# Attention of the first stretches in single fp32 matmuls instead of high and low halves

## The chip, the cores and the metric

The kernel runs on one core of a Trainium2 chip. The metric is the device time of one execution in microseconds (us). An execution's profile shows the span from the first to the last instruction on five engines: PE (TensorE, matrix products into PSUM), DVE (VectorE), ACT (ScalarE), POOL (GpSimd) and SP (SyncE, which here only issues DMAs). PEld is the weight load of PE.

## The reference

Causal attention with a bias, then two feed-forward layers whose activations differ. Batch 4, 8 heads, 576 queries, head size 64; 2304 tokens of width 512, feed-forward width 2048.

```python
scores = (q @ k.T) / sqrt(64)
cum = cumsum(maximum(s, 0))
bias = -(cum[:, None] - cum[None, :])
scores = where(causal, -1e9, scores + minimum(bias, 0))
x = softmax(scores) @ v              # heads side by side: 2304 x 512
h = x @ w_in;  g = maximum(h, 0) + log1p(exp(-abs(h)));  x = g @ w_out
h = x @ w_in2; g = P(h) / (Q(h) + 1e-6);                 out = g @ w_out2
```

P is a cubic and Q a quadratic with coefficients from the inputs. The weights arrive as 64-bit floats.

## The kernel before, in words

**Halves.** Every product is made precise by splitting its operands: hi is the value rounded to the short matmul format (F32R, written by an ACT copy), lo the rest (a subtraction on DVE or POOL). A feed-forward product takes three matmuls, hi x hi, hi x lo and lo x hi (L670 to L672, and L706 to L708). For scores, q and k (64 rows) are loaded twice, onto 128 partitions; `ht` holds hi and lo stacked for k and hi twice for q, `st` the lo of q against the hi of k, with four rows more for the bias: cum in high and low parts, and ones. So a score block takes two matmuls, of 128 and of 68 rows (L318, L319). The bias enters in the sum, q.k + 8 (cum_k - cum_q), and the mask in the softmax. V is stored as hi and lo side by side (`vs`), and the transposed P as two tiles, `pt_h` and `pt_l`, so that PV takes each block of P twice; its two 64-row results are added at the end by an ACT copy (L429) and a DVE add (L430). Matmuls of halves are given at least 256 columns, where need be with columns of zeros (the first 192 of each P tile, zeroed at L833).

**Parts.** A head's queries are cut into parts: M (queries 0 to 255), B (256 to 383), L (0 to 383) and H (384 to 575). The order (L444 to L450): batch 0's eight M, batch 0's eight pairs B and H, batch 1's eight L; then batch 1's H and batch 2's L, and last batch 2's H with batch 3's L and H. Each part goes through load_raw (DMAs of q, k and V), prep (halves), s1 and s2 (scores and softmax), t1 and t2 (transposes on PE through `ident`, evacuation), and pv. The loop at L464 to L485 writes them out as one stream, in which load_raw of a part stands two parts ahead, prep one, t1 and t2 one behind, pv two behind.

In softmax (L296 to L315) DVE adds the mask and takes the minimum, ACT takes the exponential with its sum, DVE the reciprocal, POOL multiplies P by it.

**The feed-forward part and the weights.** Layer one works on token tiles of 256, 256 and four of 448, with 16 slices ff of the width. A unit is a tile and a slice: 12 matmuls into h (L670 to L672), the activation on ACT and DVE, halves of it on ACT and POOL (L800, L802), 12 matmuls into the accumulators (L706 to L708). The two tiles of 256 share accumulators; a matmul with zeros opens each of these (L690). A weight slice is converted in two pieces per slice from 64-bit numbers: POOL (L536), ACT (L537), DVE (L538, L543), ACT (L547) and POOL (L548), from a load on SP's queue (L521); the low half is also stored to DRAM (L557) and read back when a later tile needs it (L567).

**What sets the order.** Tile's scheduler keeps each engine's program order, shifted by priorities (`ahead`); every engine takes its instructions in that order. `run_to` lets the stream of parts go on between units by fixed fractions (`GROUPS`, L913): batch 0's M parts run before the first unit, with conversions in their later half; batch 0's B and H parts within units 0 to 7, batch 1's L parts within units 8 to 31. All loads named here are on SP's one queue, in order.

**The start.** load_s0 and make_cum0 (L156 to L175) make batch 0's bias rows: DVE takes the maximum and the running sum (L166, L167), splits it (L168, L169), mixes the parts (L170, L171); ACT writes two rows each (L174); eight small DMAs put them into `st` (L215). prep_hi and prep_lo (L231 to L238) make halves of q and k by pairs of heads; the first two pairs at once, the other two before their parts. make_cum (L184 to L199) does the same for all rows and stores them in DRAM (`cum_d`), from where prep loads them by L275.

**Buffers.** `W` has 16 buffers of 4 KB per partition for weights and start tiles, `Q` 6 (raw, ht, st), `J` 4 (the P tiles), `V` 2 (vs), `R` 2 (raw V, later weights and results).

Of the kernel before, what the change touches and what calls it, by code (L numbers as in the profile page):

```python
# [54 lines left out]
def moe_chain_kernel(ctx, tc, qk0, qk, vv, s0, s, w1, w2, ab, out):  # L55
# [62 lines left out]
    class Part:  # L118
        def __init__(self, b, h, kind, rng, first):
            self.b, self.h, self.kind, self.rng = b, h, kind, rng  # L120
            self.fresh, self.first = rng is not None, first
# [7 lines left out]
    raw2, ht2, st2 = {}, {}, {}  # L129
# [26 lines left out]
    def load_s0():  # L156
        cum_t["s0"] = t_w("s0_t", [4 * H, M + 6], F32)
        nc.sync.dma_start(out=cum_t["s0"], in_=s0)

    def make_cum0():  # L160
        st, cst = cum_t["s0"][:, 0:M], cum_t["s0"][:, M:M + 6]
        one = t_w("one", [4 * H, M], F32)
        nc.vector.memset(one, 1.0)
        t = t_w("cum0", [4 * H, 4, M], F32)
        hi = t_w("cum0h", [4 * H, M], F32R)
# [40 lines left out]
    def open_pair(i):  # L206
        ht2[i] = t_w("ht2", [128, 2, 2, M], F32R)
        st2[i] = t_w("st2", [128, 2, 2, M], F32R)

    def load_cum(i):  # L210
        if i not in ht2:
            open_pair(i)
        for j in range(2):
            h = 2 * i + j
            nc.sync.dma_start(out=f(st2[i][64:68, j]), in_=f(cum_t["c"][4 * h:4 * h + 4]))  # L215

    def load_v0():
        t = t_r("v2", [128, 4, 2, 2, D], F32)
# [5 lines left out]
    def prep_v0(i):  # L224
        vr = v2["raw"][:, 2 * i:2 * i + 2].rearrange("p r c h d -> p (r c) h d")
        vs = t_v("vs2", [128, 4, 4, D], F32R)
        nc.scalar.activation(vs[:, :, 0:4:3, :], vr, AF.Copy)
        nc.vector.tensor_tensor(vs[:, :, 1:3, :], vr, f(vs[:, :, 0:4:3, :]), op=ALU.subtract)
        v2[i] = vs

    def prep_hi(i):  # L231
        nc.scalar.activation(ht2[i], raw2[i], AF.Copy)
        nc.scalar.activation(st2[i][0:64, :, 1], raw2[i][0:64, :, 1], AF.Copy)

    def prep_lo(i):
        raw, ht, st = raw2.pop(i), ht2[i], st2[i]
        nc.vector.tensor_tensor(st[0:64, :, 0], raw[0:64, :, 0], f(ht[0:64, :, 0]), op=ALU.subtract)
        nc.vector.tensor_tensor(ht[64:128, :, 1], raw[64:128, :, 1], f(ht[64:128, :, 1]), op=ALU.subtract)  # L238

    def prep_pair(i):  # L240
        if i > 1:
            prep_hi(i)
            prep_lo(i)
        ht, st = ht2.pop(i), st2.pop(i)
        if i == 2:
            prep_v0(1)
        for j in range(2):
            op_t[0, 2 * i + j] = (ht[:, j], st[:, j], v2[i // 2][:, (i % 2) * 2:(i % 2) * 2 + 2])

    def load_raw(p):  # L250
        if p.fresh:
            raw = t_q("raw", [128, 2, S], F32)
            nc.sync.dma_start(out=cols(raw, p.rng), in_=cols(qk[p.b, p.h], p.rng))
            raw_t[p] = raw
            p.vkey = (p.b, p.h // 2, p.rng)
            if p.vkey not in v_t:
                n = -(-p.rng[1] // 128) if p.rng[0] == "pre" else 5
                vr = tmp_tile("R", 2, (128, 5, 2, D))
                nc.sync.dma_start(out=vr[:, 0:n], in_=vv[p.b, p.h // 2, :, 0:n])
                v_t[p.vkey] = [vr, None, n]  # L260

    def prep(p):
# [3 lines left out]
        elif p.fresh:  # L266
# [50 lines left out]
    def scores(o, p, q0, k0, n):  # L317
        nc.tensor.matmul(o, p.ht[:, 0, q0:q0 + 128], p.ht[:, 1, k0:k0 + n], start=True, stop=False)  # L318
# [12 lines left out]
    def s1(p):  # L331
        p.stat = sb.tile([128, 3, 4], F32, tag="stat", bufs=3, name="stat")
        if p.kind in "LM":
            p.p1 = p_tile(p, "gh")
            bk = abank()
            scores(bk[:, 0:256], p, 0, 0, 256)
            scores(bk[:, 256:512], p, 128, 0, 256)
            softmax_rows(p.p1, bk, 0, 128, p.stat, 0)
            softmax_rows(p.p1[:, 128:384], bk[:, 256:512], 128, 256, p.stat, 1)
# [20 lines left out]
    def evac_pt(dst, src):  # L360
# [4 lines left out]
    def t1(p):  # L365
        p.ph, p.pl = pt_h[p.idx % 2], pt_l[p.idx % 2]
# [3 lines left out]
        if p.kind in "LM":  # L370
            for i, c0 in enumerate((256, 0, 128)):
                nc.tensor.transpose(bk[:, i * 128:(i + 1) * 128], p.p1[:, c0:c0 + 128], ident)
            evac_pt([t[:, 192:576] for t in (p.ph, p.pl)], bk[:, 0:384])
        else:
            for c in range(4):
                nc.tensor.transpose(bk[:, c * 128:(c + 1) * 128], p.p1[:, c * 128:(c + 1) * 128], ident)
            evac_pt(
                [t[:, 256:1024].rearrange("p (c q) -> p c q", c=4)[:, :, 0:128] for t in (p.ph, p.pl)],
                bk.rearrange("p (c q) -> p c q", c=4))

    def t2(p):
# [3 lines left out]
        if p.kind in "LB":  # L385
            for i in range(3):
                nc.tensor.transpose(bk[:, i * 128:(i + 1) * 128], p.p2[:, i * 128:(i + 1) * 128], ident)
            evac_pt([t[:, 576:960] for t in (p.ph, p.pl)], bk[:, 0:384])
        else:

            for i, k0 in reversed(list(enumerate((448, 0, 128, 256, 384)))):
                nc.tensor.transpose(bk[:, i * 64:(i + 2) * 64], p.p2[:, k0:k0 + 128], ident)  # L392
            evac_pt(
                [t[:, 64:1024].rearrange("p (c q) -> p c q", c=5)[:, :, 128:192] for t in (p.ph, p.pl)],
                bk[:, 64:384].rearrange("p (c q) -> p c q", c=5))

    def pv(p):
# [3 lines left out]
        for t in (p.ph, p.pl):  # L401
            if p.kind == "L":
# [24 lines left out]
        cs, qs = slice(c0, c0 + n), slice(q0, q0 + n)  # L427
        tm = tmp_tile("tmp", 1, (128, 384))
# [11 lines left out]
    def parts_of(lst, first=False):  # L440
        return [Part(b, h, k, r, first) for b, heads, kind in lst for h in heads for k, r in SPLIT[kind]]
# [18 lines left out]
    n = 0  # L460
# [222 lines left out]
    def open_acc(ph, T):  # L683
# [122 lines left out]
    if True:  # L806
# [23 lines left out]
        for i in range(2):  # L830
            for lst, nm in ((pt_h, "pth"), (pt_l, "ptl")):
                t = t_j(nm, [128, 1024], F32R)
                nc.gpsimd.memset(f(t[:, 0:192]), 0.0)  # L833
                lst.append(t)
# [217 lines left out]
```

## Time and profile before

| | |
|---|---|
| median of 3 runs | 1104.4 us (1101.86 to 1104.44) |
| span of the profiled execution | 1100.2 us |
| the profiled execution's own time | not given apart from its span |
| PE busy | 1030.3 us (94%), 5732 matmuls |
| PEld busy | 926.5 us (84%) |
| DVE busy | 825.4 us (75%), 1904 instructions |
| ACT busy | 836.6 us (76%), 1767 instructions |
| POOL busy | 488.2 us (44%), 543 instructions |
| DMA | 140.53 MB, mean 128 GB/s |
| granted clock, mean | 0.995 |

Busy time is the union of an engine's instructions; matmuls overlap, so that PE's is more than their number times their pace. "Idle before" is the idle time of the engine just ahead of an instruction, with what ended it. The granted clock is a share of 2.4 GHz.

### The profile page before, as it was taken

How to read it: one execution, taken by the hardware profiler on the slowest of the kernel's cores; microseconds unless marked ns; L12 is line 12 of the kernel's file. 1: busy time of each engine (PE TensorE's matmuls, PEld its weight loads, DVE VectorE, ACT ScalarE, POOL GpSimd, SP SyncE). 2: the span in 40 equal slices, each digit the busy share in tenths (PEclk: the TensorE clock that was granted, in tenths of full speed). 3: DMA queues.
4: the chain of work that ended last, by engine and by line, in shares of the span. 5: the costliest groups of instructions: out<-in, count | busy, mean ns of one | idle time of the engine just before them, and what ended most of it. 6: DMA issues, size and time to landing. Idle time of an engine off the chain costs nothing.

```text
span 1100.2 us, 17835 instructions
## 1 busy us (share of the span) xinstructions
PE 1030.3 (94%) x5732; PEld 926.5 (84%) x5732; DVE 825.4 (75%) x1904; ACT 836.6 (76%) x1767; POOL 488.2 (44%) x543
## 2 busy tenths in 40 slices
PE   3588889889999999999999999899999999999998
PEld 3477778789888888888999998799999999999996
DVE  6898998777888788886556677667777677776765
ACT  6698888878787788777556555688788888888885
POOL 3655576552222122221244676445445455454543
PEclk9999999999999999999999999899999999999999
DMA  6464566466555464432777974401000010000000
GB/s 227 167 221 158 181 222 217 162 205 178 166 160 158 142 205 132 154 94 66 226 235 223 323 280 149 160 1 45 13 30 29 1 58 1 29 30 1 30 1 29
DMA packets 70493, 140.53 MB, mean 128 GB/s; under 512 B 8384, under 2 KB 23904, under 8 KB 70400
## 3 DMA queue, kind: packets, MB, share of 16 engines
q1 hardware_dynamic: 68000, 135.37, 37.5%
q10 hardware_dynamic: 2400, 4.03, 1.5%
q8 instruction: 45, 0.74, 0.3%
q14 instruction: 48, 0.39, 0.1%
HBM read 112.66 MB, written 22.61 MB: 123 GB/s over the span
## 4 chain that ended last, share of the span: by engine, by line
PE 65%; DVE 5%; DMA 3%; ACT 3%; POOL 2%; issue 2%; SPq 0%; POOLq 0%; ACTq 0%; DVEq 0%
PE h L672 6%; PE h L671 6%; PE h L670 6%; PE acc L715 6%; PE acc L714 6%; PE acc L713 6%; PE at L418 3%; PE at L670 3%; PE at L672 3%; PE at L671 3%; PE acc L706 3%; PE acc L707 3%; PE acc L708 3%; PE at L318 2%; DMA raw64x<-in_w_dram 2%
## 5 line engine op out<-in xcount | busy, mean ns | idle before, releaser
L671 PE MATMUL h<-xs,w1h 128*128 128x448 f32 (+1 forms) x352 | 119.9, 341 | 1.4 <-DVE xs L640 1.4
L670 PE MATMUL h<-xs,w1h 128*128 128x448 f32 (+1 forms) x352 | 119.9, 342 | 1.3 <-DVE e L764 1.0
L707 PE MATMUL acc<-gl,w1h 128*128 128x448 f32 (+1 forms) x352 | 119.1, 338 | 1.2 <-POOL gl L802 1.2
L706 PE MATMUL acc<-gh,w1h 128*128 128x448 f32 (+1 forms) x352 | 119.7, 341 | 0.1
L672 PE MATMUL h<-xs,w1l 128*128 128x448 f32 (+1 forms) x352 | 118.8, 338 | 0.2 <-POOL w1l L548 0.2
L708 PE MATMUL acc<-gh,w1l 128*128 128x448 f32 (+1 forms) x352 | 118.4, 336 | 0.0
L715 PE MATMUL acc<-w2h,gl 128*128 128x512 f32 x288 | 113.8, 395 | 0.4 <-POOL gl L802 0.4
L713 PE MATMUL acc<-w2h,gh 128*128 128x512 f32 x288 | 113.8, 395 | 0.4 <-ACT gh L800 0.4
L714 PE MATMUL acc<-w2l,gh 128*128 128x512 f32 x288 | 113.6, 394 | 0.0
L315 POOL TENSOR_SCALAR PA<-PA,stat 128x384 f32<-128x384 f32 (+3 forms) x112 | 69.3, 622 | 97.2 <-DVE stat L314 51.9
L802 POOL TENSOR_TENSOR gl<-PA,gh 128x384 fp32r<-128x384 f32 x96 | 99.4, 1036 | 6.3 <-issue 4.0
L773 POOL TENSOR_TENSOR tc<-tc,e 128x384 f32<-128x384 f32 x48 | 51.7, 1076 | 102.7 <-ACT tc L771 102.7
L315 POOL TENSOR_SCALAR P<-P,stat 128x576 f32<-128x576 f32 x32 | 26.2, 819 | 143.2 <-DVE stat L313 50.7
L363 DVE TENSOR_TENSOR ptl<-at,pth 128x384 fp32r<-128x384 f32 (+2 forms) x108 | 60.7, 569 | 16.3 <-ACT pth L362 15.1
L312 ACT ACTIVATE PA<-PA,stat 128x384 f32<-128x384 f32 (+3 forms) x112 | 63.9, 571 | 10.3 <-DVE stat L299 9.0
L670 PEld LDWEIGHTS h<-xs,w1h 128*128 128x128 f32 x352 | 67.0, 191 | 5.5 <-DVE e L764 1.7
L671 PEld LDWEIGHTS h<-xs,w1h 128*128 128x128 f32 x352 | 66.8, 190 | 5.0 <-DVE xs L640 2.2
L707 PEld LDWEIGHTS acc<-gl,w1h 128*128 128x128 f32 x352 | 66.4, 189 | 4.9 <-POOL gl L802 2.0
L362 ACT ACTIVATE pth<-at 128x384 fp32r<-128x384 f32 (+2 forms) x108 | 53.3, 499 | 21.4 <-PE at L392 12.2
L706 PEld LDWEIGHTS acc<-gh,w1h 128*128 128x128 f32 x352 | 66.4, 189 | 3.6 <-DVE yb L736 0.5
L672 PEld LDWEIGHTS h<-xs,w1l 128*128 128x128 f32 x352 | 66.6, 189 | 3.1 <-POOL w1l L548 0.4
L708 PEld LDWEIGHTS acc<-gh,w1l 128*128 128x128 f32 x352 | 66.2, 188 | 3.0
(225 smaller groups left out, 3311.9 us busy)
## 6 DMA issues: line engine op xcount, KB each, us to landing
w1l<-l_d SPq DMA_DIRECT2D x148, 256.0 KB
raw<-in_w_dram SPq DMA_DIRECT2D x48, 512.0 KB
raw<-in_qk_dram SPq DMA_DIRECT2D x32, 384.0 KB
l_d<-w1l SPq DMA_DIRECT2D x32, 256.0 KB
raw64x<-in_w_dram SPq DMA_DIRECT2D x16, 512.0 KB
R<-in_vv_dram SPq DMA_DIRECT2D x16, 320.0 KB
raw<-in_qk_dram SPq DMA_DIRECT2D x8, 576.0 KB
out_dram<-yb SPq DMA_DIRECT2D x18, 256.0 KB
```

Source lines behind the costliest of these rows:

```text
L312: nc.scalar.activation(pt[:, 0:n], pt[:, 0:n], AF.Exp, bias=mn, scale=-1.0, accum_out=stat[:, i, 1:2])
L315: nc.gpsimd.tensor_scalar(pt[:, 0:n], pt[:, 0:n], stat[:, i, 2:3], 1.0, op0=ALU.mult, op1=ALU.mult)
L670: nc.tensor.matmul(h, wh[:, cs], xh, start=(k == 0), stop=False)
L671: nc.tensor.matmul(h, wh[:, cs], xl, start=False, stop=False)
L672: nc.tensor.matmul(h, wl[:, cs], xh, start=False, stop=(k == KD - 1))
L706: nc.tensor.matmul(o, wh[:, cs], gh, start=first and not both, stop=False)
L707: nc.tensor.matmul(o, wh[:, cs], gl, start=False, stop=False)
L708: nc.tensor.matmul(o, wl[:, cs], gh, start=False, stop=last and (not both or m % 2 == 1))
L713: nc.tensor.matmul(acc[m], gh[:, cs], wh, start=first, stop=False)
L714: nc.tensor.matmul(acc[m], gh[:, cs], wl, start=False, stop=False)
L715: nc.tensor.matmul(acc[m], gl[:, cs], wh, start=False, stop=last)
L802: eng.tensor_tensor(gl, g, f(gh), op=ALU.subtract)
```

## The change

The parts of the first three stretches (M, B and H of batch 0, L of batch 1) become "plain": q, k, V and P stay fp32 and go to the matmul as they are. Scores take one matmul of 66 or 68 rows on the loaded tile, with the bias rows loaded into it below q and k; q and k are loaded onto 64 partitions. Bias rows of the start are two for each head (cum and one) instead of four. V is loaded straight into `V` and used for both heads of a pair; the result is copied from the rows of its head (DVE). P is evacuated once, t1's by ACT and t2's by DVE, into one of four rotating `J` tiles. Column counts are no longer padded: an M or L part's first row block has 128 columns of scores, and PV takes only the columns that the mask leaves. `pt_h` and `pt_l` are made when the first part of halves needs them. The matmul that opens an accumulator multiplies the zero columns of `mask` with `mask`, in fp32.

```diff
 def load_s0():
-        cum_t["s0"] = t_w("s0_t", [4 * H, M + 6], F32)
+        cum_t["s0"] = sb.tile([2 * H, M + 4], F32, tag="tmp", bufs=1, name="s0_t")
...
 def make_cum0():
...
         nc.vector.tensor_tensor_scan(t[:, 1], one, t[:, 0], 0.0, op0=ALU.mult, op1=ALU.add)
-        nc.vector.tensor_copy(hi, t[:, 1])
-        nc.vector.tensor_tensor(t[:, 2], t[:, 1], f(hi), op=ALU.subtract)
-        nc.vector.tensor_scalar(t[:, 3], t[:, 2], cst[:, 1:2], None, op0=ALU.mult)
-        nc.vector.scalar_tensor_tensor(t[:, 3], f(hi), cst[:, 0:1], t[:, 3], op0=ALU.mult, op1=ALU.add)
-        cum_t["c"] = t_w("cumc", [4 * H, 2, M], F32R)
-        for i in range(2):
-            nc.scalar.activation(cum_t["c"][:, i], t[:, 3], AF.Identity,
-                                 scale=cst[:, 2 + 2 * i:3 + 2 * i], bias=cst[:, 3 + 2 * i:4 + 2 * i])
+        cum_t["c"] = t_w("cumc", [2 * H, 2, M], F32)
+        nc.scalar.activation(cum_t["c"][:, 0], t[:, 1], AF.Identity, scale=cst[:, 0:1], bias=cst[:, 1:2])
+        nc.vector.tensor_scalar(cum_t["c"][:, 1], t[:, 1], cst[:, 2:3], cst[:, 3:4], op0=ALU.mult, op1=ALU.add)
...
 def load_pair(i):
-        nc.sync.dma_start(out=t, in_=qk0[i])
+        nc.sync.dma_start(out=t[0:64], in_=qk0[i])
 def load_cum(i):
-            nc.sync.dma_start(out=f(st2[i][64:68, j]), in_=f(cum_t["c"][4 * h:4 * h + 4]))
+            nc.sync.dma_start(out=raw2[i][64:66, j], in_=cum_t["c"][2 * h:2 * h + 2])
 def prep_pair(i):
-        if i > 1:
-            prep_hi(i)
-            prep_lo(i)
...
+            op_t[0, 2 * i + j] = (raw2[i][0:66, j], None, v2["raw"][:, i])
 def load_raw(p):
+        if p.fresh and p.plain:
+            raw = t_q("rawp", [128, 2, S], F32)
+            nc.sync.dma_start(out=cols(raw[0:64], p.rng), in_=cols(qk[p.b, p.h, 0:64], p.rng))
+            nc.sync.dma_start(out=cols(raw[64:68], p.rng), in_=cols(cum_d[p.b * H + p.h], p.rng))
+            p.vkey = (p.b, p.h // 2, p.rng)
+            if p.vkey not in v_t:
+                n = -(-p.rng[1] // 128) if p.rng[0] == "pre" else 5
+                vr = t_v("vr", [128, 5, 2, D], F32)
+                nc.sync.dma_start(out=vr[:, 0:n], in_=vv[p.b, p.h // 2, :, 0:n])
+                v_t[p.vkey] = vr
+            op_t[p.b, p.h] = (raw[0:68], None, v_t[p.vkey])
 def prep(p):
-        elif p.fresh:
+        elif p.fresh and not p.plain:
 def scores(o, p, q0, k0, n):
+        if p.plain:
+            nc.tensor.matmul(o, p.ht[:, 0, q0:q0 + 128], p.ht[:, 1, k0:k0 + n], start=True, stop=True)
+            return
 def s1(p):
-            scores(bk[:, 0:256], p, 0, 0, 256)
-            scores(bk[:, 256:512], p, 128, 0, 256)
+            n = 128 if p.plain else 256
+            scores(bk[:, 0:n], p, 0, 0, n)
+            scores(bk[:, n:n + 256], p, 128, 0, 256)
 def evac_pt(dst, src, eng=None):
+        if len(dst) == 1:
+            if eng is nc.scalar:
+                nc.scalar.activation(dst[0], src, AF.Copy)
+            else:
+                nc.vector.tensor_copy(dst[0], src)
+            return
 def t1(p):
-        p.ph, p.pl = pt_h[p.idx % 2], pt_l[p.idx % 2]
+        if p.plain:
+            p.pt = (t_j("pt", [128, 1024], F32),)
+        else:
+            if not pt_h:
...
+                        nc.gpsimd.memset(f(t[:, 0:192]), 0.0)
...
 def pv(p):
+            if p.plain:
+                if p.kind == "L":
+                    blk = t[:, 64:960].rearrange("p (b q) -> p b q", b=7)
+                    ops.append((0, t[:, 320:704], bk[:, 0:384]))
+                    ops.append((1, blk[:, 1:6:4, :], bk[:, 128:384].rearrange("p (b q) -> p b q", b=2)))
+                    ops.append((2, t[:, 832:960], bk[:, 256:384]))
+                elif p.kind == "M":
+                    ops.append((0, t[:, 320:576], bk[:, 0:256]))
+                    ops.append((1, t[:, 192:320], bk[:, 128:256]))
+                elif p.kind == "B":
+                    for c in range(3):
+                        ops.append((c, t[:, 576 + c * 128:704 + c * 128], bk[:, 128:256]))
+                else:
+                    for c in range(4):
+                        ops.append((c, t[:, 256 + c * 192:448 + c * 192], bk[:, 64:256]))
+                    ops.append((4, t[:, 192:256], bk[:, 192:256]))
...
+        if p.plain:
+            nc.vector.tensor_copy(xt[r, p.h // 2, qs], bk[r, cs])
+            return
         tm = tmp_tile("tmp", 1, (128, 384))
...
 segs = [
-        parts_of([(0, R8, "M")], True),
-        parts_of([(0, R8, "BH")]),
-        parts_of([(1, R8, "L")]),
+        parts_of([(0, R8, "M")], True, True),
+        parts_of([(0, R8, "BH")], False, True),
+        parts_of([(1, R8, "L")], False, True),
...
 def open_acc(ph, T):
-                nc.tensor.matmul(a, pt_h[0][:, 0:128], w1_t[0][:, 0:512], start=True, stop=False)
+                nc.tensor.matmul(a, mask[:, 0:128], mask, start=True, stop=False)
...
         load_v0()
-        open_pair(0)
-        prep_hi(0)
         make_cum0()
-        prep_lo(0)
         load_cum(0)
         load_cum(1)
-        prep_hi(1)
-        prep_lo(1)
-        prep_v0(0)
```

## Rows read from the trace of the kernel before

**Rows 1.** The page: the span, and busy time of each engine.
```profile
span 1100.2 us, 17835 instructions
PE 1030.3 (94%) x5732; PEld 926.5 (84%) x5732; DVE 825.4 (75%) x1904; ACT 836.6 (76%) x1767; POOL 488.2 (44%) x543
```

**Rows 2.** Busy us of PE, PEld, DVE, ACT, POOL by stage; granted clock, DMA share, GB/s.
```profile
0.00:53.80 53.80, 24.54 (x90) 19.64 (x91) 39.83 (x118) 35.19 (x82) 27.02 (x43) 1.00 0.58 197
53.80:146.40 92.60, 78.06 (x535) 69.17 (x533) 84.55 (x240) 80.41 (x195) 52.66 (x62) 0.98 0.57 187
146.40:240.90 94.50, 82.13 (x645) 78.26 (x643) 76.62 (x191) 78.52 (x205) 61.27 (x72) 1.00 0.61 204
240.90:520.00 279.10, 276.07 (x1641) 243.19 (x1642) 223.53 (x698) 221.14 (x503) 63.52 (x97) 1.00 0.48 145
```

**Rows 3.** Chain that ended last, in order of time: start us, us, what.
```profile
207.34 0.65 POOL tc L536
...
248.19 1.19 PE at L418 x10
...
251.63 0.55 PE at L392 x5
```

**Rows 4.** Timeline of the start: start us, us, engine, line, operation.
```profile
1.92 0.26 POOL L833 MEMSET pth<- 128x192 f32 x1
...
3.66 0.28 DVE L168 CAST cum0h<-cum 32x256 fp32r<-32x256 f32 x1
...
6.34 1.08 ACT L174 ACTIVATE cumc<-cum,s_t 32x256 fp32r<-32x256 f32 x2
...
7.44 2.68 SPq L215 DMA_DIRECT2D st<-cumc  x4
...
9.55 0.55 PE L319 MATMUL acc<-st 68*128 68x256 f32 x1 [1.31 <-ACT st L233]
...
10.98 0.41 PE L318 MATMUL at<-ht 128*128 128x256 f32 x1
...
11.20 0.41 PE L319 MATMUL at<-st 68*128 68x256 f32 x1
```

**Rows 5.** Groups of ACT, 53.8 to 240.9: busy us, mean ns, idle before.
```profile
L276 ACT ACTIVATE ht<-raw 128x768 fp32r<-128x768 f32 (+1 forms) x18 | 15.8, 878 | 0.0
L362 ACT ACTIVATE pth<-at 128x384 fp32r<-128x384 f32 (+2 forms) x27 | 12.9, 485 | 1.3 <-PE at L392 0.9 <-PE at L387 0.2
...
L281 ACT ACTIVATE st<-raw 64x576 fp32r<-64x576 f32 (+1 forms) x17 | 10.2, 597 | 0.0
...
L429 ACT ACTIVATE tmp<-at 64x384 f32<-64x384 f32 (+2 forms) x16 | 6.2, 388 | 1.4 <-PE at L418 1.0
L290 ACT ACTIVATE vs<-R 128x640 fp32r<-128x640 f32 (+1 forms) x9 | 5.7, 633 | 0.0
```

**Rows 6.** Groups of DVE in the same stretch.
```profile
L363 DVE TENSOR_TENSOR ptl<-at,pth 128x384 fp32r<-128x384 f32 (+2 forms) x27 | 14.7, 552 | 1.9 <-ACT pth L362 1.7
L283 DVE TENSOR_TENSOR ht<-raw,ht 64x576 fp32r<-64x576 f32 (+1 forms) x18 | 14.5, 803 | 0.4
L282 DVE TENSOR_TENSOR st<-raw,ht 64x384 fp32r<-64x384 f32 (+2 forms) x18 | 13.7, 762 | 0.5 <-ACT ht L276 0.3
...
L291 DVE TENSOR_TENSOR vs<-R,vs 128x640 fp32r<-128x640 f32 (+1 forms) x9 | 8.8, 976 | 0.5 <-ACT vs L290 0.5
```

**Rows 7.** Groups of PE in the same stretch (one of three of each kind).
```profile
L671 PE MATMUL h<-xs,w1h 128*128 128x256 f32 x128 | 36.6, 287 | 1.0 <-DVE xs L640 1.0
...
L707 PE MATMUL acc<-gl,w1h 128*128 128x256 f32 x116 | 33.1, 286 | 1.2 <-POOL gl L802 1.2
```

**Rows 8.** Waits of PE, 0 to 250: us in total, times, longest.
```profile
PE h L318 <- DVE ht L238: 5.0, 1, 5.0
```

**Rows 9.** Timeline of SP's queue, 28 to 42.
```profile
30.51 0.33 SPq L199 DMA_DIRECT2D cum_d<-rows  x1
...
39.07 0.31 SPq L275 DMA_DIRECT2D st<-cum_d  x1
```

More of the change, by code (lines that the diff above doesn't have):

```diff
@@ L118, in moe_chain_kernel, with __init__ @@
     class Part:
-        def __init__(self, b, h, kind, rng, first):
+        def __init__(self, b, h, kind, rng, first, plain):
             self.b, self.h, self.kind, self.rng = b, h, kind, rng
-            self.fresh, self.first = rng is not None, first
+            self.fresh, self.first, self.plain = rng is not None, first, plain
     def cols(t, rng):
@@ L128, in moe_chain_kernel @@
     M = 256
-    raw2, ht2, st2 = {}, {}, {}
+    raw2 = {}
     v2 = {}
@@ L365, in t1 @@
     def t1(p):
-        p.ph, p.pl = pt_h[p.idx % 2], pt_l[p.idx % 2]
+        if p.plain:
+            p.pt = (t_j("pt", [128, 1024], F32),)
+        else:
+            if not pt_h:
+                for i in range(2):
+                    for lst, nm in ((pt_h, "pth"), (pt_l, "ptl")):
+                        t = t_j(nm, [128, 1024], F32R)
+                        nc.gpsimd.memset(f(t[:, 0:192]), 0.0)
+                        lst.append(t)
+            p.pt = (pt_h[p.idx % 2], pt_l[p.idx % 2])
         if p.kind == "B":
@@ L372, in t1 @@
                 nc.tensor.transpose(bk[:, i * 128:(i + 1) * 128], p.p1[:, c0:c0 + 128], ident)
-            evac_pt([t[:, 192:576] for t in (p.ph, p.pl)], bk[:, 0:384])
+            evac_pt([t[:, 192:576] for t in p.pt], bk[:, 0:384], nc.scalar)
         else:
@@ L377, in t1 @@
             evac_pt(
-                [t[:, 256:1024].rearrange("p (c q) -> p c q", c=4)[:, :, 0:128] for t in (p.ph, p.pl)],
-                bk.rearrange("p (c q) -> p c q", c=4))
+                [t[:, 256:1024].rearrange("p (c q) -> p c q", c=4)[:, :, 0:128] for t in p.pt],
+                bk.rearrange("p (c q) -> p c q", c=4), nc.scalar)
     def t2(p):
@@ L387, in t2 @@
                 nc.tensor.transpose(bk[:, i * 128:(i + 1) * 128], p.p2[:, i * 128:(i + 1) * 128], ident)
-            evac_pt([t[:, 576:960] for t in (p.ph, p.pl)], bk[:, 0:384])
+            evac_pt([t[:, 576:960] for t in p.pt], bk[:, 0:384])
         else:
@@ L393, in t2 @@
             evac_pt(
-                [t[:, 64:1024].rearrange("p (c q) -> p c q", c=5)[:, :, 128:192] for t in (p.ph, p.pl)],
+                [t[:, 64:1024].rearrange("p (c q) -> p c q", c=5)[:, :, 128:192] for t in p.pt],
                 bk[:, 64:384].rearrange("p (c q) -> p c q", c=5))
@@ L400, in pv @@
         ops = []
-        for t in (p.ph, p.pl):
-            if p.kind == "L":
+        for t in p.pt:
+            if p.plain:
[14 more added lines that the diff above has]
+                    ops.append((4, t[:, 192:256], bk[:, 192:256]))
+            elif p.kind == "L":
                 blk = t[:, 64:960].rearrange("p (b q) -> p b q", b=7)
@@ L417, in pv @@
         for i, (c, mv, o) in enumerate(ops):
+            vc = p.vs[:, c] if p.plain else p.vs[:, c, 2 * hd:2 * hd + 2, :]
             nc.tensor.matmul(
-                o, p.vs[:, c, 2 * hd:2 * hd + 2, :].rearrange("p a d -> p (a d)"), mv,
+                o, vc.rearrange("p a d -> p (a d)"), mv,
                 start=(i == 0), stop=(i == len(ops) - 1))
@@ L438, in moe_chain_kernel, with parts_of @@
     }
-    def parts_of(lst, first=False):
-        return [Part(b, h, k, r, first) for b, heads, kind in lst for h in heads for k, r in SPLIT[kind]]
+    def parts_of(lst, first=False, plain=False):
+        return [Part(b, h, k, r, first, plain) for b, heads, kind in lst for h in heads for k, r in SPLIT[kind]]
     R8 = range(8)
     segs = [
-        parts_of([(0, R8, "M")], True),
-        parts_of([(0, R8, "BH")]),
-        parts_of([(1, R8, "L")]),
+        parts_of([(0, R8, "M")], True, True),
+        parts_of([(0, R8, "BH")], False, True),
+        parts_of([(1, R8, "L")], False, True),
         parts_of([(1, R8, "H"), (2, R8, "L")]),
@@ L829, in moe_chain_kernel @@
             fill=NEG, base=0, channel_multiplier=1)
[L830 to L834, printed above, removed]
         prep(allp[0])
```

42 lines of the change are left out of this document (10 added, 32 removed).

## The prediction

> **What bounds the kernel now.** I read the page first: PE is busy in 94% of the span [rows 1]. That average hides the stages, so next came the table of busy time by stage [rows 2]. From 240.9 us on PE is full (276.07 of 279.10 us in the first piece of it); the changed stretches lie before that. I cut there at the opening of the accumulators and at the first unit of 448 tokens: stage A (0 to 53.8, batch 0's M parts and the first weight conversions), B (to 146.4, batch 0's B and H parts beside feed-forward units), C (to 240.9, batch 1's L parts beside more units). In B, DVE is busy 84.55 of 92.60 us, ACT 80.41, PE 78.06; in C all three stand between 76 and 83 of 94.50. No engine is full; they wait for each other. The chain that ended last shows it: at 207 us it starts from a weight conversion on POOL, from 248 us it runs through PE's own matmuls [rows 3].
>
> PE's busy time overstates its need, since matmuls overlap; their pace is what counts. Ten 256-column matmuls of halves take 1.19 us, 0.119 each, or 0.06 us per block of 128 columns; five 128-column fp32 transposes take 0.55 us, 0.11 each [rows 3]. In stage A the same 256 columns start 0.22 us apart [rows 4]: the pace of 1.2 GHz, though the granted clock of that stage says 1.00 of 2.4 GHz [rows 2]. The engine had stood idle before; that is all the rows say of why.
>
> What PE needs in B and C together: the units (128 + 116) x 3 matmuls [rows 7] x 0.119 = 87.1 us; the attention products 39.5 (a B part holds 18 blocks of halves, 6 in its scores and 12 in PV; an H part 37, an L part 28; eight of each are 664, x 0.06); 96 + 48 transposes x 0.11 = 15.8. That is 142.4 of 187.1 us, and 45 are spare.
>
> **What goes.** The copies and subtractions that make halves of q and k are L276 and L281 on ACT [rows 5], L282 and L283 on DVE [rows 6]. Of about 18 each, 15 belong to changed parts (seven B, since one is split in A, and eight L): 13.2 + 9.0 us off ACT, 11.4 + 12.1 off DVE. V's halves (L290, L291), 7 of 9: 4.4 and 6.8. ACT's copy at the end of PV goes wholly (L429; 24 at 0.39 by its largest row, 9.4). Each transposed P is evacuated once: t1 by ACT, so 16 of DVE's subtractions at 0.55 to 0.6 go, 9.4 us; t2 by DVE, so 24 of ACT's copies at 0.485 go, 11.6 us. The add L430 becomes a copy of the same columns at the same cost. ACT's 158.9 us in B and C come to about 111, DVE's 161.2 to about 121. POOL's 113.9 stay.
>
> In A, DVE's four operations from L168 at 3.66, and the wait of ACT's bias rows behind its copies of q and k, last until 6.34; one of two rows, 0.54, goes too [rows 4]. So the load of the rows leaves near 4.2 us instead of 7.44, 3.2 us of gain; from there to the matmul that reads it (9.55) nothing changes. PE's wait of 5.0 us for the split of pair 2 goes [rows 8]. Beyond that a dozen us each of DVE's 40 and ACT's 35 go; nothing is full there, so I take 4 us. A: 53.8 to about 42, **minus 12**.
>
> **What comes.** One plain fp32 matmul replaces two or more of halves. No row shows one. Per block the bounds are: from below the fp32 transpose, 0.11 us, which only moves data; from above four matmuls of halves, 0.24: the units make a precise product from three (L670 to L672), and an instruction that is told nothing of halves would have the fourth to do as well. I take 0.24, since those units are nearest in what is computed. The Trainium skill, FP8 and Floating Point Precision, section TensorE Precision Notes, says that true FP32 takes four passes; at the row's pace that gives the same sum.
>
> The blocks, no longer padded to 256 columns, are 6 per M, 6 per B, 15 per H and 12 per L. B and C: 264 x 0.238 = 62.8 for 39.5, +23.3. The four matmuls that open accumulators (L690) become fp32 of 512 columns, 0.95 for 0.24 us, the first two at half clock and so double: +4.2. In A, 48 blocks at half clock, 22.8 for 15.2, lie beside 29 us of PE's idle time [rows 2] and cost nothing; without that cover, 7.6. PE's need in B and C: 142.4 + 23.3 + 4.2 = 169.9 us.
>
> So PE becomes the engine with most to do. After 240.9, where it is that now, it is busy 99%, with DVE and ACT at 80%. The conversions are still in the way, so I take 97%: 169.9 / 0.97 = 175 for 187, **minus 12**, nearly all of it in B; C, whose units are denser, hardly moves.
>
> **Moves.** The row load L275 goes from prep into load_raw, one part earlier on SP's queue, and reads what L199 stores. The store is issued at 30.51, the first read at 39.07 [rows 9]. With A shorter the read comes at about 31, right behind the store, and weight loads (L521) and V's stand behind it. I bound this by half of that distance, 4 us of loss, or as much gain where loads come sooner, and take 0, since weights are loaded up to four conversions ahead. The zeroing of the P tiles (four memsets of 0.26 us [rows 4]) goes from the start to batch 1's first H; POOL, busy 63.52 of 279.10 us then [rows 2], covers it, and without that it is 1 us. q and k come on 64 partitions instead of 128, half the bytes; the loads were hidden already.
>
> **Sum.** Minus 12 and minus 12 are minus 24. The profiled span is 1100.2 us [rows 1]; nothing gives the time around it in that execution, and the median of the runs, 1104.4, stands 4.2 above it, the lowest 1.7. I take 4.2: 1100.2 - 24 + 4.2 = 1080.
>
> **Rivals.** *Plain fp32 is cheap* (0.15): at 0.11 per block PE needs 142.4 - 39.5 + 29.0 + 0.8 = 133 us in B and C; the fullest engine now reaches 86% (161.2 of 187.1), so they take 154, minus 33, with A's 12 near 1059. For it: the transposes read fp32 at that pace. Against: they multiply by the identity.
>
> *The conversions set the pace* (0.13): B and C stay, only A gains, 1092. For it: the chain at 207 [rows 3], and POOL's 61.27 us in C are unchanged [rows 2]. Against: POOL is far from full, and the ACT and DVE steps of a conversion queue behind less.
>
> *Slower* (0.20): the weight load of a plain fp32 matmul isn't hidden. What speaks for it is the transpose, 0.11 per block where halves take 0.06: 0.05 over. With four passes that is 0.2 us a matmul: (4 + 8 + 6) x 8 in B and C, 29 us; 199 / 0.99 = 201, +14. In A 32 matmuls at half clock, 13 us, of which I let half show: minus 6. About +8, 1112. It decides once a block costs 0.09 us more than I took (24 over 264 blocks), 0.33. Against: matmuls of halves hide theirs, at 256 columns. The Trainium skill, TensorE: Matmul & The Clock Gate, section Weight-path perf modes, says that the fast weight load is off for FP32 input; by that rule this rival holds, and no row here shows the load of a plain fp32 product.
>
> **How the numbers follow.** The forecast has 0.52 (1066 to 1094: PE at 90 to 99% in B and C, A's 4 us and the queue's 4 either way). The range takes in the upper part of cheap fp32 and the lower half of the slow case: 1055 to 1106. A measurement of this kernel tells 0.3%, 3.3 us, from no change. Faster: 0.52 + 0.15 + 0.13, less the far edges, 0.78; same 0.06; slower 0.16.
>
> **What would show it.** Right: the first scores near 6.3 us and no wait for a split of pair 2; accumulators open near 42; ACT near 63% and DVE near 69% of B and C, PE full there; a plain matmul of 256 columns paced at 0.48 us. Wrong: that pace at 0.22 (cheap) or over 0.65 (slow); PE still idle 10% of C with POOL named (conversions); PE waiting for loads of bias rows.

## The result and the profile after

The changed kernel takes 1108.3 us (median of 8 runs, 1104.9 to 1111.7), the kernel before 1103.2 in the same runs: ratio 1.0054, 95% interval 1.0038 to 1.0070. It is slightly slower; the forecast was 1080, with 1055 to 1106 as its range. The profiled execution took 1107.75 us at a span of 1106.0.

The page's span and PE's row, which answer to [rows 1]:

```profile
span 1106.0 us, 17605 instructions
PE 1052.1 (95%) x5736; PEld 937.4 (85%) x5736; DVE 774.2 (70%) x1827; ACT 789.4 (71%) x1660; POOL 480.3 (43%) x543
```

DVE lost 51 us and ACT 47, PE gained 22, POOL lost 8. The stages need boundaries that both kernels have, so I cut at the first unit's matmul, at the opening of the second token tile's accumulators, and at the first unit of 448 tokens: 55.2, 146.4 and 240.9 before; 41.7, 152.2 and 245.8 after. Busy time by these stages, after (columns as in [rows 2]):

```profile
0.00:41.74 41.74, 24.74 (x88) 19.35 (x89) 21.22 (x88) 19.85 (x54) 18.61 (x33) 0.83 0.53 170
41.74:152.24 110.50, 95.64 (x569) 79.47 (x569) 73.84 (x229) 63.15 (x156) 61.47 (x74) 0.94 0.55 174
152.24:245.80 93.56, 84.80 (x617) 78.06 (x615) 56.88 (x153) 64.76 (x168) 54.93 (x70) 0.98 0.55 182
...
245.80:525.00 279.20, 276.43 (x1646) 243.83 (x1645) 222.39 (x695) 220.44 (x501) 63.33 (x96) 1.00 0.47 143
```

And the kernel before, cut at the same events:

```profile
55.18:146.40 91.22, 76.67 (x530) 67.98 (x529) 83.37 (x235) 79.03 (x192) 51.34 (x59) 0.98 0.57 186
146.40:240.90 94.50, 82.13 (x645) 78.26 (x643) 76.62 (x191) 78.52 (x205) 61.27 (x72) 1.00 0.61 204
```

A is 13.4 us shorter (55.2 to 41.7), B 19.3 longer (91.2 to 110.5), C 0.9 shorter. The kernel before opens the second tile's two accumulators apart, at 146.4 and 149.8, the changed one both at 152.2; counted from 149.8, B is 15.9 longer and C 2.4. Either way B and C together are 18.4 longer (185.7 to 204.1), and 18.4 less 13.4 is the 5 us that the kernel lost. The last piece is as before. So the first stretch's gain arrived, and B took it all back and more, though DVE and ACT emptied there: 73.84 and 63.15 of 110.50 us, against 83.37 and 79.03 of 91.22. POOL's busy time rose by 10 us in B, and the granted clock fell to 0.94.

What came out as forecast can be read in PE's timeline after (start us, us, operation, idle before):

```profile
98.62 0.28 PE L723 MATMUL acc<-gl,w1h 128*128 128x256 f32 x1
99.23 0.77 PE L388 MATMUL at<-ident,P 128*128 128x128 f32 x5 [0.33 <-POOL P L292]
99.84 1.02 PE L296 MATMUL at<-rawp 68*128 68x512 f32 x2
100.70 1.68 PE L431 MATMUL acc<-pt,vr 128*128 128x192 f32 x10
102.27 0.55 PE L383 MATMUL at<-ident,PA 128*128 128x128 f32 x3
```

One plain matmul is two records. The scores of 512 columns (x2) hold PE from 99.84 to 100.70, 0.86 us or 0.215 per block of 128; the five PV matmuls (x10; 832 columns, 6.5 blocks) from 100.70 to 102.27, 0.242 per block. The forecast had 0.24. The transposes are at 0.12 per block ((99.84 - 99.23) / 5), near the 0.11 of [rows 3].

The same stretch on POOL and, under it, the two reciprocals on DVE whose results POOL's multiplications (L292) wait for:

```profile
98.44 0.74 POOL L292 TENSOR_SCALAR P<-P,stat 128x576 f32<-128x576 f32 x1 [2.74 <-PE h L688]
99.14 2.51 POOL L564 TENSOR_TENSOR w1l<-tc,w1h 128x512 fp32r<-128x512 f32 x2
101.62 0.59 POOL L292 TENSOR_SCALAR PA<-PA,stat 128x384 f32<-128x384 f32 x1
```

```profile
98.08 0.16 DVE L291 RECIPROCAL stat<-stat 128x1 f32<-128x1 f32 x1
...
99.13 0.16 DVE L291 RECIPROCAL stat<-stat 128x1 f32<-128x1 f32 x1
```

The first multiplication starts at 98.44, 0.20 us behind its reciprocal; the second could start at 99.29 and starts at 101.62, since two low halves of a conversion (L564) lie ahead of it. Over the 32 multiplications of B the mean wait between the reciprocal's end and the multiplication's start is 0.70 us, ten of them over 1 us; before, it was 0.43 over 29, with three. PE's longest waits in B name them (us in total, times, longest):

```profile
PE acc L383 <- POOL PA L292: 3.7, 2, 3.3
PE acc L388 <- POOL P L292: 1.7, 2, 1.4
PE at L372 <- POOL PA L292: 1.7, 1, 1.7
PE acc L431 <- DVE pt L346: 1.6, 1, 1.6
```

C's longest waits are of another kind. The first line has them; under it, ACT's timeline ahead of the longest, which ends at 204.53:

```profile
PE at L296 <- ACT pt L344: 6.9, 4, 3.4
```

```profile
200.91 0.67 ACT L553 ACTIVATE raw<-raw 128x512 f32<-128x512 f32 x1 [2.39 <-POOL tc L552]
...
203.47 0.63 ACT L563 ACTIVATE w1h<-tc 128x512 fp32r<-128x512 f32 x1 [1.32 <-DVE tc L559]
204.00 0.47 ACT L344 ACTIVATE pt<-at 128x384 f32<-128x384 f32 x1
```

The scores wait for ACT to evacuate a transposed P. PE had finished its transposes at 199.4, and ACT comes to them at 204.00, behind two steps of a conversion for whose input it stands idle 2.39 and 1.32 us. It is the same shape of wait as on POOL: a short operation that PE needs, behind a conversion in its engine's order.

In the kernel before, PE's waits in B and C had been these above all:

```profile
PE at L318 <- DVE ptl L363: 7.4, 7, 2.2
PE at L392 <- POOL P L315: 4.1, 4, 1.4
```

Summed by the engine that ended them, PE waited 15.7 us for DVE, 10.2 for POOL and 0.5 for ACT before; after, 5.0 for DVE, 11.5 for POOL and 6.9 for ACT. So the waits for DVE went, but those for the other two grew, and 26.4 us became 23.3. None of these waits after is for a converted weight itself.

More conversions lie in B than before. POOL's group of the low half there, before (first line; L548) and after (L564), with their number behind the x, busy us and mean ns:

```profile
L548 POOL TENSOR_TENSOR w1l<-tc,w1h 128x512 fp32r<-128x512 f32 x11 | 15.5, 1412 | 5.3 <-ACT w1h L547 5.3
```

```profile
L564 POOL TENSOR_TENSOR w1l<-tc,w1h 128x512 fp32r<-128x512 f32 x16 | 21.1, 1333 | 12.6 <-ACT w1h L563 12.2 <-PE acc L724 0.4
```

Before, six low halves lay ahead of the first unit and eleven in B; after, two and sixteen. The conversions' order is fixed, and a shorter A hides fewer of them.

The clock is the third loss. PE idled 1.64 us ahead of a PV at 105.90; then:

```profile
98.00:106.30 8.30, 6.33 (x39) 5.08 (x38) 4.73 (x17) 4.60 (x11) 5.74 (x8) 1.00 0.55 194
106.30:109.70 3.40, 3.40 (x15) 2.86 (x14) 2.14 (x5) 1.40 (x3) 2.63 (x2) 0.50 0.29 102
```

The granted clock goes to 0.50 (1.2 GHz) for 3.4 us after a stretch in which PE was busy 6.33 of 8.30. By the clock's means (0.94 of 110.5, 0.98 of 93.6) 8.5 us of full clock are missing in B and C, before 2; that is an estimate of the cost.

### The profile page after: what moved, and what is told of

Read it like the earlier page. It is cut to its first block, busy times and chain, and to the rows that moved or that the text cites. A ratio compares the mean times of both kernels' runs of the same rounds, so it can differ in the third digit from the quotient of the medians.

```text
span 1106.0 us, 17605 instructions
## 1 busy us (share of the span) xinstructions
PE 1052.1 (95%) x5736; PEld 937.4 (85%) x5736; DVE 774.2 (70%) x1827; ACT 789.4 (71%) x1660; POOL 480.3 (43%) x543
## 4 chain that ended last, share of the span: by engine, by line
PE 70%; DVE 9%; DMA 6%; POOL 6%; ACT 5%; issue 4%; SPq 0%; POOLq 0%; DVEq 0%; ACTq 0%
PE h L687 6%; PE h L688 6%; PE h L686 6%; PE acc L731 6%; PE acc L730 6%; PE acc L729 6%; PE at L431 4%; PE acc L722 3%; PE acc L723 3%; PE acc L724 3%; PE at L688 3%; PE at L687 3%; PE at L686 3%; DMA raw<-in_w_dram 3%; PE at L298 2%
## 5 line engine op out<-in xcount | busy, mean ns | idle before, releaser
L722 PE MATMUL acc<-gh,w1h 128*128 128x448 f32 (+1 forms) x352 | 124.0, 352 | 0.1
L686 PE MATMUL h<-xs,w1h 128*128 128x448 f32 (+1 forms) x352 | 123.2, 351 | 0.0
L687 PE MATMUL h<-xs,w1h 128*128 128x448 f32 (+1 forms) x352 | 121.7, 346 | 0.9 <-DVE xs L656 0.9
L292 POOL TENSOR_SCALAR PA<-PA,stat 128x384 f32<-128x384 f32 (+3 forms) x112 | 67.2, 603 | 95.0 <-DVE stat L291 61.1
L292 POOL TENSOR_SCALAR P<-P,stat 128x576 f32<-128x576 f32 x32 | 26.6, 832 | 145.9 <-DVE stat L290 51.7
L289 ACT ACTIVATE PA<-PA,stat 128x384 f32<-128x384 f32 (+3 forms) x112 | 63.9, 571 | 17.8 <-DVE stat L276 16.8
L731 PEld LDWEIGHTS acc<-w2h,gl 128*128 128x128 f32 x288 | 54.3, 189 | 13.6 <-POOL gl L818 0.8
L730 PEld LDWEIGHTS acc<-w2l,gh 128*128 128x128 f32 x288 | 54.4, 189 | 12.4
```

Of the source, the lines that this page charges most:

```text
L289: nc.scalar.activation(pt[:, 0:n], pt[:, 0:n], AF.Exp, bias=mn, scale=-1.0, accum_out=stat[:, i, 1:2])
L292: nc.gpsimd.tensor_scalar(pt[:, 0:n], pt[:, 0:n], stat[:, i, 2:3], 1.0, op0=ALU.mult, op1=ALU.mult)
L686: nc.tensor.matmul(h, wh[:, cs], xh, start=(k == 0), stop=False)
L687: nc.tensor.matmul(h, wh[:, cs], xl, start=False, stop=False)
L722: nc.tensor.matmul(o, wh[:, cs], gh, start=first and not both, stop=False)
L730: nc.tensor.matmul(acc[m], gh[:, cs], wl, start=False, stop=False)
```

## The experiments

The table has the boundaries of every run (first unit, opening of the second tile, first unit of 448 tokens, us) and the ratio to the kernel before, measured on the same chip. For the kernels in halves throughout, the second boundary isn't used.

| run | first unit | second tile | 448 | time | ratio (95%) |
|---|---|---|---|---|---|
| before | 55.2 | 146.4 | 240.9 | | 1 |
| the change | 41.7 | 152.2 | 245.8 | 1108.3 | 1.0054 (1.0038 to 1.0070) |
| e1 M only | 40.9 | 144.6 | 242.8 | 1105.0 | 1.0038 (1.0023 to 1.0053) |
| e2 B, H in halves | 41.1 | 148.2 | 248.5 | 1110.3 | 1.0076 (1.0061 to 1.0092) |
| e4 PV cut | 41.0 | 140.6 | 232.5 | 1091.9 | 0.9911 (0.9894 to 0.9928) |
| e5 norm on DVE | 42.2 | 140.3 | 234.5 | 1098.3 | 0.9968 (0.9952 to 0.9983) |
| e6 before, norm on DVE | 54.8 | | 254.5 | 1115.0 | 1.0107 (1.0085 to 1.0129) |
| e7 e5, L in halves | 41.2 | 142.0 | 238.9 | 1100.5 | 0.9976 (0.9965 to 0.9987) |
| e8 norm on ACT | 47.6 | 142.4 | 237.6 | 1097.3 | 0.9943 (0.9924 to 0.9961) |
| e9 low half on DVE | 40.8 | 138.5 | 229.3 | 1090.4 | 0.9885 (0.9866 to 0.9904) |
| e10 before, low half on DVE | 49.9 | | 239.7 | 1099.8 | 0.9988 (0.9973 to 1.0004) |
| e11 e9 and e8 | 43.6 | 138.7 | 228.4 | 1088.8 | 0.9889 (0.9873 to 0.9906) |
| e12 V loaded later | 38.2 | 150.2 | 246.4 | 1106.3 | 1.0052 (1.0033 to 1.0071) |
| e13 e9, norm of B to L on ACT | 40.6 | 134.9 | 224.7 | 1086.5 | 0.9859 (0.9838 to 0.9881) |
| e14 conversions earlier | 42.8 | 158.6 | 257.1 | 1117.6 | 1.0134 (1.0107 to 1.0160) |
| e15 e13 and e14 | 41.8 | 138.4 | 231.6 | 1094.5 | 0.9930 (0.9903 to 0.9956) |

**One part of the change at a time.** e1 keeps the plain form for M alone, e2 for M and L; the parts of halves need zeros in 576 columns of each P tile.

```diff
-        parts_of([(0, R8, "BH")], False, True),
+        parts_of([(0, R8, "BH")]),
-        parts_of([(1, R8, "L")], False, True),      # e1 only
+        parts_of([(1, R8, "L")]),
```

> Batch 0's M parts stay plain; batch 0's B and H parts and batch 1's L parts go back to halves (the P tiles of halves are zeroed over 576 columns instead of 192). Theory P, the plain products of B and H cost PE in stage B what the start had gained: the first unit stays near 42 us and B and C take their times of before (95 and 91 us), so about 13 us under before, 1087 to 1094. Rival Q, something that isn't in those products (weight conversions, weight loads) paces stage B, so that an earlier start is taken back whatever the products are: the accumulators of the second tile open at 147 to 150 us as before, 1100 to 1105.

> M and L parts plain, B and H in halves. Theory P: stage C costs 2 to 4 us more than before, since PE's extra passes there are nearly paid for by fewer waits: 1089 to 1097, 2 to 4 us above the kernel with M alone. Rival Q: 1102 to 1109. If L's plain products are a gain in themselves, it lies below the kernel with M alone.

e1: the start is 14.3 us earlier than before (55.2 to 40.9). At the opening of the second tile 1.8 us of it is left, at the first unit of 448 tokens nothing (242.8 against 240.9), with all B, H and L parts in halves as before. The plain passes of B and C can't be what took it. B and C of e1 (columns as above):

```profile
40.91:144.62 103.71, 82.00 (x538) 71.59 (x538) 87.69 (x243) 82.29 (x194) 63.15 (x70) 0.94 0.58 187
144.62:242.82 98.20, 85.09 (x646) 81.04 (x645) 77.32 (x193) 81.58 (x215) 63.14 (x73) 0.97 0.64 205
```

POOL's 63.15 us stand against 51.34 before, 15 low halves against 11, and PE's waits in B for POOL's multiplications are 13.7 us against 8.8. By its time e1 lies at the upper edge of rival Q's range, and e2 1 us above it; both are far from theory P. e2 against e1 makes L plain: 0.4% slower. Against the change it differs by B and H: no gain from those two being plain that the intervals separate.

**PE's passes.** e4 leaves out the products of all key blocks but the first in PV of the plain parts.

```diff
+        if p.plain:
+            ops = ops[:1]
```

> The changed kernel, in which PV of the plain parts takes only the first key block and leaves out the others: 7168 columns less of plain products in stage B and 3072 in C, 4 passes each at 2.4 GHz: 11.9 and 5.1 us less for PE. Theory P (PE's passes are on the path): 1108 less 14 to 17, 1091 to 1094. Rival S (the stages are as long as the chain of waits from scores to transposes, and PE's passes fill idle time): less than 5 us of it shows, 1103 to 1108.

1091.9, 16.4 below the change, as theory P has it: what PE does more lies on the path too. A stage that waits for an engine in one place and for PE in the next is shortened by both.

**POOL's multiplication.** e5 moves the normalisation (L292) of the plain parts to DVE.

```diff
-        nc.gpsimd.tensor_scalar(pt[:, 0:n], ...)
+        eng = nc.vector if plain else nc.gpsimd
+        eng.tensor_scalar(pt[:, 0:n], ...)
```

> The changed kernel with the division of P by its sum on DVE instead of POOL in the plain parts. In stages B and C PE's longest waits are for POOL's multiplication (transposes of P) or for what follows on it. Rival S (PE waits because POOL's multiplication queues behind weight conversions): 8 to 15 us less than the changed kernel, 1093 to 1100. Theory P alone: PE is what is full, and only the waits of a few us go: 1103 to 1108.

1098.3, in rival S's range and faster than both kernels. The mean wait of a multiplication behind its reciprocal in B falls from 0.70 to 0.36 us. B and C of e5:

```profile
42.19:140.31 98.12, 89.99 (x569) 74.61 (x568) 83.49 (x259) 61.91 (x155) 38.96 (x42) 0.99 0.67 198
140.31:234.51 94.20, 85.80 (x616) 78.27 (x615) 65.74 (x168) 63.91 (x166) 48.65 (x54) 0.98 0.55 174
```

B is 12.4 us shorter (110.50 to 98.12), and its clock is back at 0.99.

e6 makes the same move in the kernel before (in its first three stretches); e7 is e5 with L in halves; e8 puts the multiplication on ACT; e9 leaves it on POOL and takes the conversions' low half, which stands ahead of it, to DVE.

```diff
-        nc.gpsimd.tensor_scalar(pt[:, 0:n], ...)
+        g = sum(pos[0] >= m for m in marks[0:4])        # e6, on the kernel before
+        eng = nc.vector if g < 3 else nc.gpsimd
+        eng.tensor_scalar(pt[:, 0:n], ...)
...
-        parts_of([(1, R8, "L")], False, True),          # e7, on e5
+        parts_of([(1, R8, "L")]),
...
+        if plain:                                       # e8
+            nc.scalar.activation(pt[:, 0:n], pt[:, 0:n], AF.Copy, scale=stat[:, i, 2:3])
+            return
...
-        nc.gpsimd.tensor_tensor(lo, t, f(hi), op=ALU.subtract)
+        (eng or nc.gpsimd).tensor_tensor(lo, t, f(hi), op=ALU.subtract)   # e9; conv passes nc.vector
```

> The kernel before, with the normalisation of P on VectorE instead of GpSimd in the first three stretches (all halves stay, the outputs are the same sum). Theory room (the move pays only because the plain form emptied VectorE: in B before it was busy 86.8 of 94.6 us, and 30 multiplications of 0.6 us add 17): no gain or a loss, 1102 to 1115 us. Rival queue (GpSimd's late multiplication bounds both kernels alike): the 10 us that the same move gained behind the change, 1090 to 1097.

> Plain matmuls in the first two stretches only, with their normalisation on VectorE; the third stretch (first 384 queries of batch 1) in halves, normalised on GpSimd as before. Theory passes (in the third stretch PE's four passes cost more than the emptier engines give back: with the first stretch alone plain, the kernel was 5 us faster than with the first and the third): 1088 to 1096 us. Rival (with the normalisation out of GpSimd's queue the third stretch pays too): 1098 to 1106.

> The changed kernel with the normalisation of P on ScalarE in the plain parts, instead of GpSimd. Theory queue (it is GpSimd's place in the chain, behind the conversions, that makes the waits; any engine with room does): 1094 to 1101 us, near the 1098 on VectorE. Rival (VectorE is the right place because the reciprocal just ahead is its own, and ScalarE is in the chain on both sides): 1104 to 1110.

> The changed kernel with the low half of the first matrix's converted weights (128x512, 1.3 us each on GpSimd, 32 of them) subtracted on VectorE; the normalisation stays on GpSimd. Theory queue (the multiplications stand behind the conversions on GpSimd): 1096 to 1102 us, most of what moving the multiplications gave. Rival (the multiplication's own place and length on GpSimd make the wait, not what is ahead of it): 1105 to 1112.

e6 is 1.1% slower, at the upper end of what theory room expects. From the first unit to the 448-token units its DVE is busy 180.90 of 199.66 us, and PE's clock falls to 0.91:

```profile
54.80:254.46 199.66, 169.76 (x1172) 157.57 (x1170) 180.90 (x478) 161.34 (x402) 82.17 (x82) 0.91 0.56 181
```

e7 misses theory passes: L in halves or plain makes no difference that the intervals separate, once the multiplication is off POOL. e8 and e9 are as theory queue has it, e9 beyond its range (1096 to 1102 expected, 1090.4 measured). A low half that takes POOL 1.28 us takes DVE 0.68 (the group of L564 in B of e9; min, median and max in ns):

```profile
L564 DVE TENSOR_TENSOR w1l<-tc,w1h x16: 671/684/1083, 43.2 to 131.9; 128x512 fp32r<-128x512 f32 x16
```

The multiplication stayed on POOL here and is no shorter (0.64 us on average for a PA tile in B, 0.60 after the change), and its mean wait in B fell from 0.70 to 0.32 us: it was what stood ahead of it in the queue.

**Controls, the start, and both moves.** e10 is e9's edit in the kernel before; e11 is e8's and e9's together; e12 moves load_v0 behind the rows of the first two pairs.

```diff
         load_pair(1)
-        load_v0()
         make_cum0()
         load_cum(0)
         load_cum(1)
+        load_v0()                                       # e12
```

> The kernel before (all halves) with the low half of the first matrix's converted weights subtracted on VectorE instead of GpSimd. Theory room (the move pays only behind the change, because VectorE was busy 86.8 of 94.6 us in B before and 73.8 of 110.2 in B after): no gain or a loss, 1101 to 1112 us. Rival queue (GpSimd's queue bounds the kernel before as well): most of the 18 us that the same move gained behind the change, 1084 to 1092.

> The changed kernel with both moves: the conversions' low half on VectorE, the normalisation of P in the plain parts on ScalarE, so that GpSimd has of the first three stretches the conversions' first multiplication and the units' low half alone. Theory chain (what is left of PE's waits behind GpSimd's multiplications, 6.2 us in the stretches B and C of the run with the low half on VectorE, goes too): 1080 to 1087 us. Rival (the first stretch is longer with the normalisation on ScalarE, 47.6 us against 40.8 to the first unit's matmul, and the rest gives nothing more): 1089 to 1097.

> The changed kernel with the load of batch 0's V issued behind the rows of the first two pairs instead of ahead of them. The rows of the first pair landed 4.4 us after their issue at 4.12, against 2.1 before. Theory queue at the start (V's transfer ahead of them is what delays the rows): first score matmul at 6.3 to 7.3 us instead of 8.66, and no difference in the time that can be measured, 1104 to 1109 us, as B takes the gain of A back. Rival (four row transfers on one another, or the weights' load): first score matmul at 8.3 to 9.0.

e10: no gain that can be measured, 0.9988, though the first unit comes 5.3 us earlier. In halves DVE had little room for it (169.44 of 189.82 us busy between the boundaries); behind the change it is worth 1.7% of the time (1.0054 to 0.9885). e11, at 1088.8, lies between its two expectations: PE's waits for POOL's multiplications are gone, but the first unit comes 2.8 us later than in e9, as the rival had it, if by less. e12: the first score matmul comes at 7.40 instead of 8.66, between the two expectations, so V's transfer was part of the delay. Another part is a weight load (L537, issued at 3.09) that the changed kernel has ahead of the rows: in e1 and e2, where it comes behind them and V stays ahead, the first scores are at 7.78 and 7.76. In e12 the first unit comes 3.6 us earlier (41.7 to 38.2), B has 16 low halves as in the change, and the time is the same within the intervals, 1106.3. Here too a gain of the start did not arrive.

**The better version.** e13 is e11 with M's multiplications back on POOL.

```diff
-            softmax_rows(..., plain=p.plain)
+            softmax_rows(..., plain=p.plain and not p.first)
```

> As the run with both moves (low half of the conversions on VectorE, normalisation on ScalarE), but the first stretch normalises on GpSimd, so that ScalarE takes the multiplications of the second and third stretch alone. Theory chain (the first unit's matmul comes back from 43.6 to 41 us, and the stretch B, in which PE was busy 90.2 of 93.1 us with both moves, cannot shorten further): 1085 to 1089 us. Rival (the earlier start is taken back in B once more): 1088 to 1092.

1086.5 us, 1.4% faster than the kernel before and 22 us faster than the change. Its interval overlaps those of e9 and e11, so it isn't shown to be faster than these. Its B and C, and PE's longest waits in them:

```profile
40.58:134.91 94.33, 88.58 (x568) 74.79 (x568) 78.80 (x244) 78.81 (x188) 21.36 (x26) 0.99 0.66 210
134.91:224.67 89.76, 85.23 (x616) 78.35 (x615) 63.78 (x169) 70.36 (x185) 29.27 (x40) 0.98 0.57 183
```

```profile
PE at L299 <- ACT pt L347: 2.8, 4, 1.7
PE at L391 <- ACT P L293: 2.3, 2, 1.3
```

No wait for POOL is left among them.

**Do the conversions' places matter?** e14 (on the change) and e15 (on e13) spread the first stretch's eight conversions over the whole of it.

```diff
-S_START = 2
+S_START = 1
```

> The changed kernel with its eight conversions of the first stretch spread over the whole of it, instead of its second half. After the change only 2 conversions' low halves lie ahead of the first unit's matmul (6 before) and 16 between it and the opening of the second token tile (11 before). Theory displaced (the start's gain is taken back because conversions that the longer first stretch had hidden now stand in GpSimd's queue of B): the first unit at 41 to 44 us with 5 to 7 low halves ahead of it, and 1095 to 1103 us. Rival (where the conversions lie does not matter, B is long for PE's own passes): 1105 to 1111.

> The same spread in the version with the low half on VectorE and the later normalisations on ScalarE. Theory displaced (GpSimd's queue is no longer in the way there, so that it matters little where the conversions lie): 1083 to 1089 us. Rival (the conversions' whole chain, not GpSimd's queue, sets B): 1074 to 1082.

Both are slower than the kernel they start from, by 9 and 8 us, outside all expectations. The edit didn't do what it was for: POOL's first conversion starts at 22.66 us instead of 23.93, three low halves instead of two end ahead of the first unit, and the accumulators open 9 us later (47.6 to 56.6). Only two low halves fewer lie in e14's B (14 for 16), and B is 5.3 us longer all the same (42.8 to 158.6). So it hardly tests the displacement, and what it shows does not speak for it. That more conversions lie in B is counted in the trace, and that their low halves delay the multiplications is shown by e9; that B would have kept the 13 us with the conversions where they were is argued, not shown.

## Why the prediction was wrong

**What held.** The start: A was to lose 12 us, and the first unit came 13.4 earlier. Two smaller marks missed: the first scores at 8.66 instead of 6.3 (the rows' transfer took 4.4 us, partly for V and a weight load, by e12, e1 and e2), and the opening at 47.56 instead of 42, since it now comes behind the first units. PE's wait for the split of pair 2 [rows 8] is gone. ACT's and DVE's relief came: ACT 157.5 to 127.9 us in B and C, DVE 160.0 to 130.7, though four conversions more lie there; the shares, 63% and 64%, were forecast as 63% and 69%. That the shares agree is luck: 48 and 40 us were to go, 30 and 29 went, and B and C are 204 us long instead of 175. The forecast took off whole lengths, while the operations of an engine overlap: ACT's in B and C before add up to 186.7 us in 157.5 of busy time.

**The price held.** 0.215 us per block in scores and 0.242 in PV, against 0.24. Cheap fp32 and the slower rival both fall. The Trainium skill, FP8 and Floating Point Precision, section TensorE Precision Notes, gives four passes; the trace agrees: 512 columns at 2.4 GHz are 0.213 us, and the matmul took 0.86. The Trainium skill's rule that the fast weight load is off for FP32 input (TensorE: Matmul & The Clock Gate, section Weight-path perf modes), by which the slower rival would hold, hardly shows as time: at the scores' pace PV's 6.5 blocks would take 1.40 us and took 1.57, so 0.17 us over five matmuls, 0.03 each and not 0.2. The time came out near that rival's 1112, but for another reason.

**The step that failed** is "I take 97%: 169.9 / 0.97 = 175 for 187, minus 12". It takes for granted that PE's 45 us of waiting vanish when ACT and DVE empty. B and C took 204.1 us: PE's 169.9 and 34 besides, where the forecast had 5. PE's idle time there only fell from 26.9 to 23.6 us, while its busy time rose from 158.8 to 180.4. Of the 34, 23.3 are waits (11.5 for POOL, 6.9 for ACT, 5.0 for DVE) and about 8.5 the half clock. I had read POOL as far from full, 61 of 94.50 in C, and let that count against the conversions. But POOL takes its instructions in order, and a multiplication of 0.6 us that every part needs stands behind low halves of 1.3; the length of the queue ahead, not the busy share, sets the wait. e9 and e5 show it: the same PE work in 188.6 and 192.3 us (229.3 - 40.8, 234.5 - 42.2) instead of 204.1, with PE's instructions untouched. In e9 the waits are 13.1 us (6.2 for POOL, 3.5 for ACT) and the time at half clock 5.9 us instead of 16.8; 10.2 us less of waits and half of the 10.9 us less at half clock account for the 15.5 by which B and C are shorter. The rival that named the conversions was nearest in its mechanism, but it had B and C stay and let A's gain stand (1092). In fact B and C grew, by PE's passes (e4) beside waits that hardly shrank, and A's gain was lost, in e1 and e12 too. Why an earlier start is lost where B, H and L are as before (e1) stays open: the longer waits for POOL's multiplications there are counted, but no run held the conversions where they were.

**What a PE bound gives.** With POOL out of the way, e13 takes 184.1 us in B and C, 92% of it PE's 169.9 us. So even there 97% is not reached: some 2.7 us of full clock are missing (0.99 of 94.3, 0.98 of 89.8), and PE still waits for evacuations and for ACT's multiplication. A minus 14.6, B and C minus 1.6: together 16 off the 1102.3 of the kernel before in the same runs, which is the 1086.5. It lies within the 1066 to 1094 of the forecast, but that was made for another kernel.

**Smaller terms.** I took 4.2 us around the span; the profiled execution after has 1.75, so the sum started about 2.5 too high, if the kernel before has no more. The store of the bias rows is issued at 34.66 us and their first read at 40.21, 5.6 apart, and no wait of PE in B or C is for a load. The 1.00 of the first stretch in [rows 2] is no reading: that trace's record of the clock begins at 57.08 us, and there the spacing of 256-column matmuls goes from 0.21 to 0.12. The changed kernel's record begins at 21.0 and has half clock from 27.8 to 44.9 us.

## What to carry to other kernels

Emptying the two fullest engines can be worth nothing in itself where a third, half idle, stands in the chain with an in-order queue: look at how long a short operation that everything needs waits behind long ones that nothing needs yet. A change that trades an engine's time for PE's may pay only with a second move into the room it made (1.0054 alone, 0.9885 with it), and the move alone may pay nothing (0.9988): test it with and without. And a shorter first stage need not keep its gain: look where the work goes that it used to hide. That this work took the gain here is argued, not shown.

## What the runs showed of the hardware

A plain fp32 matmul stands in the trace as two matmul records, each of twice its columns in cycles: 0.86 us for 512 columns at 2.4 GHz. The subtraction of 128x512 into F32R took POOL 1.28 us and DVE 0.68. PE's granted clock was 0.50 (1.2 GHz) for 3.4 us each in four stretches of B and C after the change (from 55.1, 106.3, 120.0 and 205.3 us). Each begins less than 1 us behind the end of an idle time of PE, of 3.30, 1.64, 1.02 and 3.35 us. Idle times of 1.3 to 1.7 us that end at 65.2, 71.4, 87.2 and 167.5 are followed by no fall, so the length of one wait alone does not tell. With the low half on DVE (e9), or the multiplication (e5), no such stretch is left between 44 and 213 us, and one follows at 213.9 and 217.9. So some waits of PE cost more there than their own length, and the relief brought more than the wait.
